# Loading the last three chunks of x by partition quadrant

## Chip, cores and metric

One core of one Trainium2 chip. The time is device microseconds of one execution, as the median of several; the kernel before takes 575.4 us.

## The reference, cut to what matters

```python
# x: (1, 384, 384, 384) bf16, dw: (1, 1, 384), pw: (384, 384)
out = x * dw[0, 0]                                  # k = 1: a depthwise scale per channel
return jnp.einsum('bhwc,cd->bhwd', out, pw)         # 147,456 rows times a 384 x 384 matrix
```

113 MB are read and 113 MB written. The kernel folds the scale into the weights, so each row of x needs only a transpose and a matrix product.

## The kernel before

The rows are cut into 288 supertiles of 512 rows. A chunk is a run of supertiles loaded by one transfer; most chunks have ten, the last group has 3, 2, 1, 1 and 1.

```python
head, tail = [[1, 1, 2, 2, 4]], [[6, 4], [3, 2, 1, 1, 1]]   # supertiles per chunk, by group
...
def load_x(t):
    g, i, off, first, L = chunks[t]
    dst = Xs[g % NR][:, 4 * off : 4 * (off + L), :]          # NR = 3 buffers
    rows = xf[512 * first : 512 * (first + L), :]
    if first + LONG < NS:                                     # LONG = 3, NS = 288
        src = rows.rearrange("(p s) c -> p (s c)", p=P)
        dst = dst.rearrange("p s c -> p (s c)")
    else:                                                     # the last three chunks
        src = rows.rearrange("(a k q) c -> q a k c", k=4, q=4)
    if i == 0 and g >= NR:                                    # buffer free?
        je = g_end[g - NR]
        nc.sync.wait_ge(s_t[je % 2][1], je // 2 + 1)
    nc.sync.dma_start(dst, src).then_inc(s_x[g % NR][i], 16)
```

VectorE transposes a supertile (two instructions), TensorE multiplies it (48 matmuls that each use 32 partitions, in twelve steps of four, one for each of four PSUM banks), ScalarE copies the result to an output buffer (VectorE helps with half of the very last), and SP stores each chunk once its last copy is done. The three last chunks have rows interleaved over the four quadrants of 32 partitions, so that their stores can write 3072 bytes in a piece; their loads then move 768-byte runs.

## Time and profile before

| | before |
|---|---|
| median of three runs | 575.39 us (575.29 to 575.57) |
| span of the profiled execution | 573.7 us |
| TensorE busy | 567.3 us, idle 0.1 us ahead of the main matmuls |
| DMA | 226.9 MB, 395 GB/s |

The lines that carry the reading stand in the prediction.

### The profile page before, as it was taken

The numbers are of one execution on the slowest core, as the hardware profiler recorded it, in microseconds if no ns is written. First come the engines' busy times: TensorE is split into PE (matmuls) and PEld (weight loads), VectorE is DVE, ScalarE is ACT, GpSimd is POOL, SyncE is SP. The second block draws the span as 40 slices with busy tenths as digits, with TensorE's granted clock in tenths as the row PEclk, the third lists the DMA queues.
The fourth block names the chain that finished last, engine by engine and source line by source line (L and its number), as shares of the span: only waits on it lengthen the run. The fifth ranks groups of instructions, "written<-read, shape, count | busy, mean of one in ns | idle before, by whom it ended". The sixth has DMA issues, their size and how long they took to land.

```text
span 573.7 us, 29706 instructions
## 1 busy us (share of the span) xinstructions
PE 567.3 (99%) x13869; PEld 414.9 (72%) x13869; DVE 509.3 (89%) x583; ACT 418.8 (73%) x296; POOL 0.9 (0%) x8
## 2 busy tenths in 40 slices
PE   8999999999999999999999999999999999999996
PEld 5777777777777777777777777777777777777774
DVE  6899999999999999999999999999999999999994
ACT  6777777777777777777777777777777777777775
POOL 0000000000000000000000000000000000000000
PEclk9999999999999999999999999999999999999999
DMA  8999999999999999999999999999999999994996
GB/s 324 432 409 417 430 397 430 444 424 422 399 408 416 384 397 436 398 383 395 432 398 384 395 429 390 393 401 429 402 385 419 401 390 397 425 394 149 402 408 251
DMA packets 25912, 226.88 MB, mean 395 GB/s; under 512 B 1197, under 2 KB 5678, under 8 KB 22062
## 3 DMA queue, kind: packets, MB, share of 16 engines
q1 hardware_dynamic: 25900, 226.79, 98.0%
q14 instruction: 9, 0.07, 0.0%
q8 instruction: 1, 0.02, 0.0%
q10 hardware_dynamic: 2, 0.00, 0.0%
HBM read 113.54 MB, written 113.25 MB: 395 GB/s over the span
## 4 chain that ended last, share of the span: by engine, by line
PE 98%; DMA 1%; ACT 0%; DVE 0%; issue 0%; SPq 0%
PE ps L166 97%; DMA pw_n<-in_pw_dram 1%; PE ps L216 1%; DMA out_dram<-O 0%; ACT O L307 0%; DVE O L304 0%; SPq L337 0%; SPq L100 0%
## 5 line engine op out<-in xcount | busy, mean ns | idle before, releaser
L166 PE MATMUL ps<-w_r,T 32*128 32x384 bf16 x13824 | 561.8, 321 | 0.1
L258 DVE STREAM_TRANSPOSE T<-X 128x384 uint32<-128x384 uint32 x576 | 506.2, 882 | 54.0 <-DMA X<-in_x_dram 2.4
L307 ACT CAST O<-ps 128x1536 bf16<-128x1536 f32 x288 | 413.5, 1436 | 147.9 <-PE ps L166 147.9
L166 PEld LDWEIGHTS ps<-w_r,T 32*128 32x128 bf16 x13824 | 412.9, 93 | 149.2 <-issue 0.7
L271 ACT CAST w_r<-ps 128x768 bf16<-128x768 f32 x5 | 3.7, 805 | 1.7 <-PE ps L216 1.6
L183 PE MATMUL ps<-zero 32*128 32x384 bf16 x24 | 2.6, 494 | 1.4 <-POOL zero L232 1.4
L304 DVE CAST O<-ps 128x768 bf16<-128x768 f32 x1 | 1.0, 958 | 3.0 <-DMA out_dram<-O 3.0
L216 PE MATMUL ps<-pw_n,sel_w 64*128 64x384 bf16 x18 | 3.0, 510 | 0.1
L183 PEld LDWEIGHTS ps<-zero 32*128 32x128 bf16 x24 | 0.7, 100 | 2.6 <-issue 2.6
L216 PEld LDWEIGHTS ps<-pw_n,sel_w 64*128 64x128 bf16 x18 | 1.2, 138 | 1.6 <-issue 1.2
L244 ACT ACT_TABLE_LOAD x1 | 1.3, 1283 | 1.5 <-SPq L100 1.5
L276 DVE TENSOR_REDUCE sel<-eye 128x64 f32<-128x128 bf16 x1 | 0.3, 290 | 1.8 <-POOL eye L234 1.8
L271 DVE CAST w_r<-ps 128x768 bf16<-128x768 f32 x1 | 1.0, 956 | 1.0 <-PE ps L216 1.0
L286 DVE TENSOR_SCALAR sel_w<-sel,dw_f 128x256 bf16<-128x256 f32 x3 | 0.9, 348 | 0.0
L283 DVE COPY dw_f<-ps 128x3 f32<-128x3 f32 x1 | 0.2, 161 | 0.8 <-PE ps L198 0.8
L198 PEld LDWEIGHTS ps<-ones,dw_row 1*128 1x128 bf16 x3 | 0.2, 98 | 0.2 <-issue 0.2
L244 ACT COPY warm<-warm 128x1 f32<-128x1 f32 x2 | 0.3, 188 | 0.0
L234 POOL TENSOR_SCALAR_AFFINE_SELECT eye<-ones 128x128 bf16<-128x128 bf16 x1 | 0.3, 292 | 0.1
L232 POOL MEMSET zero<- 128x192 uint32 x1 | 0.3, 258 | 0.0
L198 PE MATMUL ps<-ones,dw_row 1*128 1x1 bf16 x3 | 0.2, 159 | 0.0
L233 POOL MEMSET ones<- 128x128 bf16 x1 | 0.2, 204 | 0.0
L231 POOL MEMSET warm<- 128x3 f32 x1 | 0.1, 101 | 0.5 <-SPq L100 0.5
(4 smaller groups left out, 0.4 us busy)
## 6 DMA issues: line engine op xcount, KB each, us to landing
X<-in_x_dram SPq DMA_DIRECT2D x26, 3840.0 KB, 21.5
out_dram<-O SPq DMA_DIRECT2D x26, 3840.0 KB, 27.5
X<-in_x_dram SPq DMA_DIRECT2D x2, 1536.0 KB, 17.4
out_dram<-O SPq DMA_DIRECT2D x2, 1536.0 KB, 13.7
X<-in_x_dram SPq DMA_DIRECT2D x3, 768.0 KB, 8.8
out_dram<-O SPq DMA_DIRECT2D x3, 768.0 KB, 8.9
X<-in_x_dram SPq DMA_DIRECT2D x1, 2304.0 KB, 18.9
out_dram<-O SPq DMA_DIRECT2D x1, 2304.0 KB, 12.1
```

Source lines behind the costliest of these rows:

```text
L166: mm = nc.tensor.matmul(PS[s][:, q, :D], lhsT=Ts[s][32 * q : 32 * q + 32, b, par::2], rhs=w_r[32 * q : 32 * q + 32, b, par, :], start=(b, ...
L183: nc.tensor.matmul(PS[0][:, i, :D], lhsT=zero[32 * i : 32 * i + 32, 0:P], rhs=zero[32 * i : 32 * i + 32, :], start=True, stop=True, tile_p ...
L198: mm = nc.tensor.matmul(PS[1][:, 0, D + k : D + k + 1], lhsT=dw_row[:, P * k : P * k + P], rhs=ones[0:1, 0:1], start=True, stop=True,)
L216: mm = nc.tensor.matmul(PS[(k + 1) % 2][:, 2 * r + v, :D], lhsT=sel_w[64 * v : 64 * v + 64, k, r, :, :].rearrange("p q w -> p (q w)"), rhs ...
L232: nc.gpsimd.memset(zero[:].bitcast(U32), 0).then_inc(s_zero)
L234: nc.gpsimd.affine_select(out=eye[:], in_=ones[:], pattern=[[-1, P]], compare_op=mybir.AluOpType.is_equal, fill=0.0, base=0, channel_multi ...
L244: c = nc.scalar.copy(warm[:, s + 1 : s + 2], warm[:, 0:1])
L258: ins = nc.vector.transpose(out=Tw[:, 3 * h : 3 * h + 3], in_=Xw[:, :, j, 96 * h : 96 * h + 96].rearrange("p k (b w) -> p b k w", w=32),)
L271: o = nc.vector.tensor_copy(out, in_) if e == 0 else nc.scalar.copy(out, in_)
L286: nc.vector.tensor_scalar_mul(sel_w[:, k], sel[:].unsqueeze(2).to_broadcast([P, 2, 4, 32]), dw_f[:, k : k + 1]).then_inc(s_sw)
L304: e = nc.vector.tensor_copy(Ov[:, nq:4, j, :], PS[s][:, nq:4, :D])
L307: a = nc.scalar.copy(Ov[:, 0:nq, j, :], PS[s][:, 0:nq, :D])
```

## The change

Intent: each of the three loads used an access pattern with a dimension of 4 slowest; loading the quadrants one by one lets 32 partitions be slowest, so that all DMA engines share the work.

```diff
+    x_count = []
+    for t, (g, i, off, first, L) in enumerate(chunks):
+        n = 4 if first + LONG >= NS else 1
+        x_count.append(16 * n + max([... earlier count on the same semaphore ...], default=0))
...
             else:
                 src = rows.rearrange("(a k q) c -> q a k c", k=4, q=4)
-            nc.sync.dma_start(dst, src).then_inc(s_x[g % NR][i], 16)
+                for q in range(4):
+                    nc.sync.dma_start(dst[32 * q : 32 * q + 32], src[q]).then_inc(sem, 16)
...
-                    nc.vector.wait_ge(s_x[g % NR][i], 16 * sum(...))
+                    nc.vector.wait_ge(s_x[g % NR][i], x_count[t])
```

More of the change, by code (lines that the diff above doesn't have):

```diff
@@ L60 @@
     NT = len(chunks)
+    x_count = []
+    for t, (g, i, off, first, L) in enumerate(chunks):
+        n = 4 if first + LONG >= NS else 1
+        x_count.append(16 * n + max([x_count[u] for u in range(t) if chunks[u][0] % NR == g % NR and chunks[u][1] == i], default=0))
     g_end = [max(c[3] + c[4] for c in chunks if c[0] == g) - 1 for g in range(len(groups))]
@@ L104, in load_x @@
             rows = xf[512 * first : 512 * (first + L), :]
-            if first + LONG < NS:
-                src = rows.rearrange("(p s) c -> p (s c)", p=P)
-                dst = dst.rearrange("p s c -> p (s c)")
-            else:
-                src = rows.rearrange("(a k q) c -> q a k c", k=4, q=4)
+            sem = s_x[g % NR][i]
             if i == 0 and g >= NR:
@@ L112, in load_x @@
                 nc.sync.wait_ge(s_t[je % 2][1], je // 2 + 1)
-            nc.sync.dma_start(dst, src).then_inc(s_x[g % NR][i], 16)
+            if first + LONG < NS:
+                src = rows.rearrange("(p s) c -> p (s c)", p=P)
+                nc.sync.dma_start(dst.rearrange("p s c -> p (s c)"), src).then_inc(sem, 16)
+            else:
+                src = rows.rearrange("(a k q) c -> q a k c", k=4, q=4)
+                for q in range(4):
+                    nc.sync.dma_start(dst[32 * q : 32 * q + 32], src[q]).then_inc(sem, 16)
         def store(t):
@@ L256, in transposes @@
                 if h == 0 and j == 0:
-                    nc.vector.wait_ge(s_x[g % NR][i], 16 * sum(len(ls) > i for ls in groups[g % NR : g + 1 : NR]))
+                    nc.vector.wait_ge(s_x[g % NR][i], x_count[t])
                 ins = nc.vector.transpose(
```

## The prediction

> **What bounds the kernel now.** I read the page of the kernel before from the top: the busy table, then the costliest groups.
>
> ```profile
> PE 567.3 (99%) x13869; PEld 414.9 (72%) x13869; DVE 509.3 (89%) x583; ACT 418.8 (73%) x296; POOL 0.9 (0%) x8
> ...
> L166 PE MATMUL ps<-w_r,T 32*128 32x384 bf16 x13824 | 561.8, 321 | 0.1
> L258 DVE STREAM_TRANSPOSE T<-X 128x384 uint32<-128x384 uint32 x576 | 506.2, 882 | 54.0 <-DMA X<-in_x_dram 2.4
> L307 ACT CAST O<-ps 128x1536 bf16<-128x1536 f32 x288 | 413.5, 1436 | 147.9 <-PE ps L166 147.9
> ```
>
> The number to see is the last of the matmul row: TensorE was idle 0.1 us ahead of 13,824 matmuls. A busy figure alone would prove little, but ScalarE, which copies each result out, waited 147.9 us for these matmuls and for nothing else, while VectorE waited 2.4 us for x in the whole run. One supertile (512 rows of x, 48 matmuls) costs 561.8 / 288 = 1.951 us of TensorE, against 2 x 0.882 = 1.764 us of VectorE and 1.436 us of ScalarE. TensorE is the bound, from 7.2 us to the end.
>
> The change touches three loads late in the program, so next I read the stretch around them by windows, and the queue of the issuing engine (SP) in order of time. Columns of the windows: stretch, length, busy time and instruction count of each engine, granted clock, DMA share, GB/s.
>
> ```profile
> 0.00:518.00 518.00, 516.37 (x12621) 377.65 (x12625) 464.89 (x533) 380.59 (x269) 0.93 (x8) 1.00 1.00 406
> 518.00:530.00 12.00, 12.00 (x304) 8.83 (x300) 10.80 (x13) 8.63 (x6) 0.00 (x0) 1.00 0.37 118
> 530.00:560.00 30.00, 30.00 (x745) 22.11 (x741) 27.24 (x31) 22.32 (x16) 0.00 (x0) 1.00 0.98 397
> 560.00:562.00 2.00, 2.00 (x59) 1.49 (x52) 1.80 (x3) 1.49 (x2) 0.00 (x0) 1.00 0.39 152
> ```
>
> ```profile
> 512.29 0.71 SPq L113 DMA_DIRECT2D X<-in_x_dram  x1
> 513.05 8.79 SPq L113 DMA_DIRECT2D X<-in_x_dram  x1
> 521.89 4.44 SPq L113 DMA_DIRECT2D X<-in_x_dram  x1
> 526.38 4.41 SPq L128 DMA_DIRECT2D out_dram<-O  x1
> 535.37 0.39 SPq L128 DMA_DIRECT2D out_dram<-O  x1
> ```
>
> Here is the defect that the change repairs. The three loads of 384 KiB took SP 0.71, 8.79 and 4.44 us to issue, where other issues take 0.33 to 0.39, and they held the store behind them back to 526.38. For 12 us the DMA engines moved 118 GB/s at 0.37 of their capacity. TensorE was busy 12.00 of those 12.00 us all the same, at clock 1.00.
>
> **What the Trainium skill says.** "DMA: Bandwidth & Descriptors", section "Why a DMA increments its semaphore by 16 and not by 1": an SP transfer runs on k engines, k being the largest number up to 16 that divides the slowest dimension of both access patterns, and k engines post the completion. The old source has q, size 4, slowest, so k = 4; the new one has a = 32, its destination 32 partitions, so k = 16. The trace agrees on the 4: the page's DMA line counts the tiny packets.
>
> ```profile
> DMA packets 25912, 226.88 MB, mean 395 GB/s; under 512 B 1197, under 2 KB 5678, under 8 KB 22062
> ```
>
> The DMA view lists 38 loads of x, 38 stores, one of pw and one of dw: 78 transfers. If 74 post on 16 engines, the three loads on 4 and the one-row dw on 1, that is 74 x 16 + 3 x 4 + 1 = 1197, exactly the count. With k = 16 for the three it would be 1233.
>
> Same page, "Rules for kernel authors": two transfers to disjoint partition halves serialize because each already sprays over all engines; use one. Splitting would thus gain nothing if the old load had used 16 engines; it gains here only through k.
>
> "TensorE: Matmul & The Clock Gate", section "Wait — 56ns, not 53.3ns?": warm start-to-start is N / 2.4 GHz + 2.5 ns. With N = 384 that is 162.5 ns; and "TensorEngine Tiling (Array Packing)", "Key Properties", says that tiles operate independently, so four 32-row matmuls share one such interval. An estimate from the two pages: 48 / 4 x 162.5 = 1950 ns per supertile. The trace has 1951. The bound engine has no slack that a better transfer could return.
>
> **The change part by part.**
>
> Removed: three issues that take 0.71 + 8.79 + 4.44 = 13.94 us of SP, and about 4 us more (4.41 - 0.37) of the store behind them, which I take to be back-pressure of four full queues. A check: 393,216 bytes in 4.44 us is 89 GB/s, 22% of the 397 GB/s of a good stretch, close to 4 engines of 16.
>
> Added: twelve issues of 96 KiB, with the same bytes in the same 768-byte runs. At 0.35 us each (the usual issue of a load) that is 4.2 us, so SP is through at about 512.3 + 4.2 = 516.5; at 0.71 each, 520.8. I expect the first, as each transfer now puts 512 / 4 / 16 = 8 data packets on a ring, not 128. The three chunks are 1.18 MB: at 400 GB/s, 2.9 us, instead of about 12. SP saves about 10 us around 512 to 526. The tiny packets become (74 + 12) x 16 + 1 = 1377.
>
> Moved: the wait of VectorE counts 64 instead of 16 on each chunk's semaphore, still one wait. The store at 526.38 belongs to supertiles 250 to 259. The last copy-out begins at 569.00 and copies come every 1.95 us, so the one of supertile 259 began at 569.00 - 28 x 1.95 = 514.4 and ended at 515.8. That store goes out 5 to 10 us sooner.
>
> Who waited for any of this?
> - VectorE for x. The last transpose starts at 565.1, two per supertile, so the first of the last three chunks (supertile 285) is transposed from about 565.1 - 2 x 1.95 - 0.97 = 560.2. The slow stretch ended near 530: some 25 to 30 us to spare before the change.
> - ScalarE for the output buffer. Supertile 280 reuses the buffer that the delayed store empties. Its copy started at 569.00 - 7 x 1.95 = 555.4; the store landed 18.1 us after 526.38, at 544.5. Spare: 10.9 us.
> - The later stores, from 535.37 on, go out when a copy is done, so TensorE sets them.
>
> Saved on the path to the end: 0. Added: 0.
>
> The end itself: the last copy-out on VectorE starts at 569.01 and takes 0.96, the last store is issued at 570.06 and lands 2.3 us later, and the span closes at 573.7. None of these pieces changes if the last stores find empty queues. They did before: at 560 to 562 the DMA share was down to 0.39, so the backlog of the stall had been worked off 8 us before the last store. The change only empties it sooner.
>
> Sum: 575.39 + 0 = 575.4 us.
>
> **The rivals.**
>
> *The end was held by the store backlog, and comes sooner.* For it: SP is freed about 10 us earlier, and the page's chain names a store (2.46 us) near the end, for which the last VectorE copy is said to have waited 3.0 us. Against it: that copy waits for a store of three groups back, landed at 544.5, and for TensorE; it began within 0.01 us of the ScalarE copy that shows TensorE as its releaser. And the 0.39 share at 560. If true: 1 to 5 us less, 570 to 574.
>
> *Full-speed DMA beside the compute slows VectorE or TensorE.* For it: 118 GB/s becomes about 400 in this stretch. Against it: TensorE was fully busy and the copies came every 1.95 us at 118 and at 397 GB/s alike; and bytes only move from one time to another. If true for 12 us by a few per cent: 0.3 us more.
>
> *The twelve issues cost SP more than the three.* For it: nine more instructions; a queue that is full of the preceding loads could hold each up. Against it: even 1.2 us apiece would only equal the old 13.94 us, and nothing on the path waits for SP there. If they took 25 us, which nothing suggests, the store would slip past the copy at 555.4: up to some us more.
>
> *A straggling engine delays landing anyway.* The two ordinary loads just ahead landed 17.3 and 18.7 us after issue, so some queue holds old work. Then the split loads land near 530 whatever their width. Hidden too, but the gain in landing would be smaller than the gain in issue time.
>
> **Range and chances.** Three runs lay within 575.29 to 575.57. Predicted 575.4; I allow 0.5 us below and above for another chip or moment and for the small rivals: 574.9 to 575.9. Beyond 2% means under 563.9 or over 586.9. The first is about TensorE's own 561.8 us with a start and an end of 2 us together, and these take 7.2 and 4.7; the second needs a stall of 11 us that no part of the sum contains. Faster 0.01, same 0.98, slower 0.01.
>
> **What would show it right or wrong.** Right: twelve issues of about 0.35 us between 512 and 517, none above 1.5; no stretch near 118 GB/s from 518 to 530; the store now at 516 to 521; 1377 packets under 512 B; matmul idle time still 0.1 us; 1.95 us between copies; the last store still issued at 570.1. Wrong: idle time of TensorE beyond 0.5 us, a VectorE wait for x late in the run, a ScalarE wait for a store, or a last landing that moves by over 1 us. A count of 1233 or of 1197 would refute the engine arithmetic though not the time.

## More of the kernel before

One more line, from the waits of the issuing engine (SP), is the measure that will matter. Its columns: who waits, at which line, for whom, then microseconds in total, how often, and the longest.

```profile
SPq L141 <- DMA out_dram<-O: 2.0, 1, 2.0
```

It is SP's final wait for the stores to land, after the last one was issued at 570.06.

## The result

| | before | change |
|---|---|---|
| median of six runs | 575.44 us (575.29 to 576.12) | 577.56 us (577.10 to 577.62) |
| span of the profiled execution | 573.7 us | 575.4 us |
| ratio | | 1.0033, 95% interval 1.0020 to 1.0046 |

A ratio is the mean time of one kernel's fast runs over that of the other's of the same rounds, so it is not quite the ratio of the medians. The profiled execution of the change was its shortest, 577.10, which is why the spans differ by 1.7 us and the medians by 2.1. The change is slower by 2.1 us: within 2%, as the chances said, but clear of the noise and outside the predicted range of 574.9 to 575.9.

The profile after, in the same order as before. First the page's costliest group and its DMA line:

```profile
L173 PE MATMUL ps<-w_r,T 32*128 32x384 bf16 x13824 | 562.0, 321 | 0.2 <-ACT w_r L278 0.2
...
DMA packets 26092, 226.88 MB, mean 394 GB/s; under 512 B 1377, under 2 KB 5858, under 8 KB 22242
```

TensorE is as before. There are exactly the 1377 tiny packets foretold, so each quadrant does run on 16 engines. Next the windows and SP in order of time:

```profile
518.00:530.00 12.00, 12.00 (x304) 8.88 (x299) 10.87 (x13) 8.64 (x6) 0.00 (x0) 1.00 0.51 130
530.00:560.00 30.00, 30.00 (x746) 22.20 (x741) 27.07 (x32) 22.19 (x16) 0.00 (x0) 1.00 0.97 394
560.00:562.00 2.00, 2.00 (x57) 1.50 (x52) 1.81 (x3) 1.49 (x2) 0.00 (x0) 1.00 0.17 63
```

```profile
512.48 0.70 SPq L120 DMA_DIRECT2D X<-in_x_dram  x1
...
516.37 2.57 SPq L120 DMA_DIRECT2D X<-in_x_dram  x1
518.98 2.31 SPq L120 DMA_DIRECT2D X<-in_x_dram  x1
521.98 4.59 SPq L120 DMA_DIRECT2D X<-in_x_dram  x1
...
528.90 0.59 SPq L135 DMA_DIRECT2D out_dram<-O  x1
...
570.20 0.33 SPq L135 DMA_DIRECT2D out_dram<-O  x1
```

The stall between 518 and 530 is still there, at 130 GB/s instead of 118. Issues still block, up to 4.59 us, though the loads now use every engine, and the held store goes out at 528.90, not sooner than before (526.38) but 2.5 us later, though its own issue is shorter (0.59 us, not 4.41), so that it is out at 529.5 and not at 530.8. Then the end. The last store is issued at 570.20 instead of 570.06; what grew is SP's wait for the stores, and the time from issue to landing. The lines below are the same store in the DMA view (kilobytes, microseconds to landing), before and then after, and after's final wait:

```profile
out_dram<-O SPq DMA_DIRECT2D x1, 384.0 KB, 2.3
```

```profile
out_dram<-O SPq DMA_DIRECT2D x1, 384.0 KB, 3.8
```

```profile
SPq L148 <- DMA out_dram<-O: 3.5, 1, 3.5
```

So 1.5 us of the 1.7 us in the spans is a last landing that takes longer, and 0.14 us a copy that ends later.

Why does 384 KB take 1.5 us longer with nearly empty queues (a mean share of 0.17 at 560)? The trace also holds the time of every increment of a store's semaphore, the counter by which a transfer reports that it is done. Sixteen engines post one each, so a transfer has sixteen completion times. For the last store, relative to the start of the span (these are read from the trace's records, not from a view of the profile):

```
            first    15th     16th
before      572.20   572.34   572.37
change      572.35   572.51   574.05
```

Fifteen engines of the change finish within 0.2 us of those before. One is late. The records don't name the engines, but the late completions of the five stores of the last group, 569.33, 571.25, 572.20, 573.13 and 574.05, lie 1.92, 0.95, 0.93 and 0.92 us apart, in proportion to one engine's share of these stores (49 KB, then 24.6 KB each). One engine is working without a pause on a backlog of its own. Looking back over the run, the lag of the sixteenth completion behind the fifteenth, at the time of the first:

```
time, us    97    125   201   299   406   500
before      0.9   3.5   6.1   7.9   8.1   9.2
change      0.7   3.1   6.5   7.6   7.0   8.0
```

(For the change the columns lie within 1 us of these times.) The lag is not the change's doing. In both kernels one engine falls behind by 7 us between 97 and 299, and then stays some 7 to 9 us late until the traffic thins out.

**Theory T.** One engine of the sixteen is slow and brings a backlog to the end. Before, the three loads ran on four engines, and the slow one was not among them: it was spared 3 x 24.6 = 73.7 KB, a little over 3 us of its time at the 23 GB/s that it makes (147 KB in 6.35 us; an engine's mean share of the 394 GB/s from 530 to 560 is 24.6, so "slow" means some 6%), and just caught up with the last store. Spreading the loads over all engines gives it its sixteenth again. Of those 3 to 4 us, what exceeds its slack is seen at the end. Four engines are not free either: in the kernel before each of them carries 295 KB of the three chunks, and the store that lands at 553.60 there has five late completions (551.23, 552.15, 552.57, 552.59 and 553.60, the others by 550.73), where the change has one. They all catch up by the last store; which of the five is the last to do so, the records don't say.

**Rival R.** Twelve small transfers instead of three, with their issues and completions, cost the time.

### The profile page after: what moved, and what is told of

The parts are those of the page before. It is cut to its first block, busy times and chain, and to the rows that moved or that the text cites. A ratio compares the mean times of both kernels' runs of the same rounds, so it can differ in the third digit from the quotient of the medians.

```text
span 575.4 us, 29715 instructions
## 1 busy us (share of the span) xinstructions
PE 567.4 (99%) x13869; PEld 417.7 (73%) x13869; DVE 508.1 (88%) x583; ACT 419.2 (73%) x296; POOL 0.9 (0%) x8
## 2 busy tenths in 40 slices
DMA packets 26092, 226.88 MB, mean 394 GB/s; under 512 B 1377, under 2 KB 5858, under 8 KB 22242
## 4 chain that ended last, share of the span: by engine, by line
PE 98%; DMA 0%; ACT 0%; DVE 0%; issue 0%; POOL 0%; POOLq 0%; SPq 0%
PE ps L173 97%; PE ps L190 0%; DMA out_dram<-O 0%; PE ps L223 0%; ACT O L314 0%; DVE O L311 0%; ACT w_r L278 0%; POOL zero L239 0%; POOL warm L238 0%; PE ps L205 0%; POOLq L344 0%; SPq L105 0%
```

## The experiments

All kept TensorE's work as it is, and the last store was issued between 569.89 and 570.85 in all of them, so that at most 0.8 us of any loss comes ahead of it. "Last wait" is SP's final wait for the stores in the profiled execution, to be held against 2.0 us before and 3.5 us in the change.

### e1_slots: twelve transfers, on four engines

```diff
-                src = rows.rearrange("(a k q) c -> q a k c", k=4, q=4)
-                for q in range(4):
-                    nc.sync.dma_start(dst[32 * q : 32 * q + 32], src[q]).then_inc(sem, 16)
+                src = rows.rearrange("(a k q) c -> k q a c", k=4, q=4)
+                for k in range(4):
+                    nc.sync.dma_start(dst[:, k, :], src[k]).then_inc(sem, 16)
```

> The last three chunks in twelve transfers again, but one per slot k instead of one per quadrant, so that q (size 4) is the slowest dimension of the source and each should run on 4 engines: same bytes, same 768-byte runs, same number of issues as the change, result correct. Theory T (one DMA engine runs about 5 us behind the others in the tail, and the change put 3 x 24.6 KB more on it): as before, 575.4 us, last store landing about 2.3 us after issue; tiny packets 74 x 16 + 12 x 4 + 1 = 1233. Rival R (twelve small transfers and their completions cost the time): as the change, about 577.5.

Measured: 575.45 us (575.29 to 576.49), the kernel before 575.52 beside it, ratio 1.0001 (0.9989 to 1.0013); correct. 1233 tiny packets as expected.

```profile
SPq L148 <- DMA out_dram<-O: 2.0, 1, 2.0
```

Twelve transfers are free as long as they stay on four engines. As the cause by itself, R is out.

### e2_wide: three transfers, on sixteen engines

```diff
-                src = rows.rearrange("(a k q) c -> q a k c", k=4, q=4)
-                for q in range(4): ...
+                src = rows.rearrange("(k p) c -> p k c", p=P)
+                nc.sync.dma_start(dst, src).then_inc(sem, 16)
```

> One transfer per chunk as before, in 768-byte runs, but with the 128 partitions as the slowest dimension of the source, so that it runs on 16 engines; the rows land in other partitions, so the result is wrong on purpose in the last 1536 rows. Theory T: as the change, 577.3 to 577.7, last landing 3.5 to 4 us after issue; tiny packets 77 x 16 + 1 = 1233. Rival R (number of transfers): as before, 575.4.

Measured: 576.69 us (576.32 to 577.03), ratio 1.0018 (1.0006 to 1.0030); wrong in the last rows.

```profile
SPq L147 <- DMA out_dram<-O: 3.1, 1, 3.1
```

With no more transfers than before, sixteen engines are slower than four by 1.2 us. The direction is T's, R would have had 575.4; but the size is a miss, 0.6 us under what I had expected. The last experiments return to that.

### e3_fifteen: is it the sixteenth engine?

```diff
                 for q in range(4):
-                    nc.sync.dma_start(dst[32 * q : 32 * q + 32], src[q]).then_inc(sem, 16)
+                    for lo, hi in ((0, 30), (30, 32)):
+                        nc.sync.dma_start(dst[32 * q + lo : 32 * q + hi], src[q, lo:hi]).then_inc(sem, 16)
```

> As the change, but each quadrant in 30 + 2 partitions, which should run on 15 and on 2 engines, so that the sixteenth engine gets none of the three chunks; 24 transfers, result correct. Theory T with the slow engine being the sixteenth: as before, 575.4, last landing near 2.3 us, and the issues no longer blocked (all under 1 us); tiny packets 74 x 16 + 12 x 17 + 1 = 1389. T with another slow engine: as the change or slightly more, 577.5 to 577.8. Rival R: above the change, about 579.5, as there are 21 extra transfers and not 9.

Measured: 577.37 us (576.80 to 577.40); correct; 1389 tiny packets, so the engine counts are as supposed. The last wait was 3.9 us, and issues still blocked, up to 1.83 us. Sparing the sixteenth engine brings nothing, and 24 transfers are no worse than 12. It was a guess at the engine, and it missed.

### e4_two and e5_one: smaller doses

Two, then one, of the three chunks by quadrant; the rest in one transfer on four engines as before.

```diff
-        n = 4 if first + LONG >= NS else 1
+        n = 4 if NS - LONG <= first < NS - LONG + 2 else 1      # e5_one: + 1
...
+                if first < NS - LONG + 2:                        # e5_one: + 1
+                    (four transfers by quadrant)
+                else:
+                    nc.sync.dma_start(dst, src).then_inc(sem, 16)
```

> The first two of the three chunks by quadrant on 16 engines, the third in one transfer on 4 as before; a dose of two thirds. Theory T: the slow engine would be done at about 570.95 us if it never waited (574.05 minus 3.1 for 73.7 KB) and the last store cannot land before 572.4, so the first 1.4 us of extra work are free and the rest shows in full: two thirds of 3.1 is 2.1, so +0.6 to +1.1, 576.0 to 576.5. Rival R (cost in proportion to extra transfers, 6 of 9): +1.4, 576.8.

> Only the first of the three chunks by quadrant, the other two on 4 engines: a dose of one third. Theory T: with two thirds the last landing was 573.46 us, with all three 574.05, so one third should be at or a little above the floor of 572.4: 575.4 to 576.1. Rival R (3 extra transfers of 9): 576.1.

Measured: two chunks 576.56 us (576.31 to 576.92), last wait 3.1 us; one chunk 575.60 us (575.34 to 576.21) beside 575.34, last wait 2.0 us. Against the kernel before beside them the three doses cost 0.26, 1.04 and 1.9 to 2.3 us: the first third is free within the noise, the others are not. A slack followed by a rise is what T needs. But the interval of e5_one (ratio 0.9989 to 1.0017) also holds the 0.7 us that a cost per transfer would have given, so the doses alone do not separate the two; e1_slots does.

### f1_seven, f2_thirteen, f4_nine, g1_four, g2_five, g3_six: which engine, and does sparing it elsewhere help?

The change is kept whole. An earlier load, the 1152 KB first chunk of the last group, is cut by partitions so that it uses only some engines.

```diff
+                dst = dst.rearrange("p s c -> p (s c)")
+                for lo, hi in ((0, 124), (124, 128)) if first == NS - 8 else ((0, P),):
+                    nc.sync.dma_start(dst[lo:hi], src[lo:hi]).then_inc(sem, 16)
```

(124 + 4 is g1_four; the others are 125 + 3, 114 + 6 + 6 + 2, 119 + 7 + 2, 63 + 63 + 2 and 117 + 11; `n` for that chunk counts its pieces.) "DMA: Bandwidth & Descriptors", section "Why a DMA increments its semaphore by 16 and not by 1", adds that an SP transfer takes the lowest-numbered k engines. If so, each cut loads a known engine with a known share. The counts of tiny packets (1369 to 1385) agree with the number of engines supposed for each piece; which engines they are, no record shows.

> The change kept whole; instead an earlier load, of 1152 KB (the first chunk of the last group), is cut into 119 + 7 + 2 partitions, which should run on 7, 7 and 2 engines, so that engines 8 to 16 get none of it. Theory T: if the slow engine is one of those nine, it loses 73.7 KB, which is what the change gave it, and the time is back at 575.4 with a last landing near 2.3 us, though the last three chunks are still split. If the slow engine is the fifth to seventh, it gets 84 KB more and the time rises to 580 to 581. Rival R (number of transfers, or the splitting itself): 577.5 or a little more.

> As the seven-engine run, but the load in 117 + 11 partitions on 13 and 11 engines. Theory T: slow engine the fourteenth to sixteenth: 575.4; slow engine earlier: 577.5 to 578.3, as it gets some 10 to 20 KB more than in the change. Rival R: 577.5.

> As the seven-engine run, but the load in 63 + 63 + 2 partitions on 9, 9 and 2 engines. Theory T: slow engine the tenth or later: 575.4; slow engine the eighth or ninth: it gets 131 KB instead of 73.7, 57 KB more, at 23 GB/s 2.5 us, so 579.5 to 580.5. Rival R: 577.5.

> The change kept whole, and the 1152 KB load in 124 + 4 partitions, both on 4 engines, so that only the first four carry it. Seven, nine and thirteen engines all made it slower, with one late engine alone, which leaves the fifth to seventh engine as the slow one, if a transfer takes the lowest-numbered engines. Theory T: that engine loses 73.7 KB, as much as the change gave it: back to 575.3 to 576.0, last landing 2.3 to 2.8 us, although the three chunks stay split on 16 engines. Rival R2 (any cutting of loads here, and any further transfer, costs time; the seven-engine run was slow for that): 577.5 or above.

> As the four-engine run, with 125 + 3 partitions on 5 and 3 engines. Theory T: slow engine the fifth: 236 KB instead of 73.7, 162 KB more, 7 us: 584 to 586; slow engine the sixth or seventh: 575.3 to 576.0.

> As the four-engine run, with 114 + 6 + 6 + 2 partitions on 6, 6, 6 and 2 engines. Theory T: slow engine the seventh: 575.3 to 576.0; the sixth: 194 KB instead of 73.7, 120 KB more, 5.2 us: 582 to 584; the fifth: the same 582 to 584.

Measured, with the share of the fifth engine in that load (one partition is 9216 bytes; 117 over 13 engines and 11 over 11 put 9 + 1 = 10 on it, and so on):

| run | engines used | on the fifth engine | median us (range) | last wait us |
|---|---|---|---|---|
| g1_four | 4 | 0 | 575.75 (575.23 to 577.66) | 4.2, see below |
| the change (g4_change) | 16 | 8 x 9216 = 74 KB | 577.60 (576.54 to 577.84) | 4.3 |
| f2_thirteen | 13, 11 | 10 x 9216 = 92 KB | 578.72 (578.26 to 580.30) | 4.7 |
| f4_nine | 9, 9, 2 | 14 x 9216 = 129 KB | 580.26 (579.72 to 580.52) | 6.2 |
| f1_seven | 7, 7, 2 | 18 x 9216 = 166 KB | 581.67 (581.10 to 582.66) | 7.4 |
| g3_six | 6, 6, 6, 2 | 21 x 9216 = 194 KB | 581.90 (581.17 to 582.27) | 8.1 |
| g2_five | 5, 3 | 25 x 9216 = 230 KB | 583.37 (582.54 to 584.59) | 8.7 |

g4_change ran beside the g runs; the f runs are from another chip, where the change made 577.35 later (h3_change). The lines for the largest of these, g2_five, and for f1_seven:

```profile
SPq L150 <- DMA out_dram<-O: 8.7, 1, 8.7
```

```profile
SPq L150 <- DMA out_dram<-O: 7.4, 1, 7.4
```

Every cut from thirteen engines down to five costs more time, and the cut to four brings it back. No count of pieces gives that order, and one engine's load does: the fifth carries a part of the load in all cuts but that to four, and the time follows its bytes. Between the change and g2_five, on one chip, 156.7 KB cost 5.77 us, 27 GB/s; between the change (577.35 on that chip) and f1_seven 92.2 KB cost 4.32 us, 21 GB/s. The smallest step is out of proportion: the 18 KB of f2_thirteen cost 1.4 us there, which bytes alone do not account for. In f1_seven's completion times, fifteen engines are done with the last store by 572.70 and one at 578.06. My sizes for single cuts were off by up to 0.7 us either way (f1_seven and f2_thirteen above the stated range, g2_five and g3_six below).

g1_four's profiled execution was its one long run, 577.66; the other four lie between 575.23 and 575.81. Its completion times show several late engines, the last done at 574.62; they may be the four that carry 295 KB each of that one load. So it was repeated with less burden on these.

### i1_four_small: the same relief with a smaller load

As g1_four, with the 768 KB load (`first == NS - 5`) cut into 124 + 4 partitions.

> The change kept whole, and the 768 KB load before the three chunks (not the 1152 KB one) in 124 + 4 partitions on the first four engines. Theory T: the slow engine loses 49 KB, 2.1 us at 23 GB/s, against the 1.7 us of the change's profile, so the time is back at 575.3 to 575.9 and the last landing at 2.3 to 2.6 us; the four engines carry 147 KB more each instead of 221. Rival R2 (further cutting only adds): 577.5 or above.

Measured: 575.71 us (575.54 to 575.98), the kernel before 575.59, ratio 0.9999 (0.9986 to 1.0013); correct.

```profile
SPq L150 <- DMA out_dram<-O: 2.7, 1, 2.7
```

The three chunks are still split on sixteen engines, there is one transfer more than in the change, and the loss is gone. The last landing took 3.0 us in the profiled run, the slowest of its five: one engine still at 572.94 beside the others at 572.2; I had expected 2.3 to 2.6.

### g4_change, h1_wide12, h2_wide, h3_change: what is left over

Why did e2_wide cost only 1.2 us? The change and the wide run were repeated, and the wide pattern was issued as twelve transfers, one per slot:

```diff
+                src = rows.rearrange("(k p) c -> k p c", p=P)
+                for k in range(4):
+                    nc.sync.dma_start(dst[:, k, :], src[k]).then_inc(sem, 16)
```

> The change itself once more, beside the others on one chip. 577.1 to 577.7, last landing 3.5 to 4 us, 15 of 16 engines done with the last store 1.5 us earlier.

> Twelve transfers of 96 KB, each over all 128 partitions on 16 engines in 768-byte runs; the rows land in other partitions, so the result is wrong on purpose in the last 1536 rows. Bytes on the slow engine as in the change; tiny packets 74 x 16 + 12 x 16 + 1 = 1377. If the number of transfers on the slow engine makes the gap to the wide run: as the change, 577.3 to 577.7. If the 32-partition shape makes it: as the wide run, 576.5 to 576.9.

> The wide run once more (three transfers on 16 engines, wrong on purpose). If the gap is real: 576.5 to 576.9, some 0.9 us under the change on the same chip; if it was the chip: within 0.3 us of the change.

> The change once more beside them: 577.4 to 577.7, as on two occasions before.

Measured: the change 577.60 (576.54 to 577.84) and 577.35 us (576.96 to 577.53); the wide run again 576.44 (576.22 to 576.80); twelve wide transfers 576.71 (576.15 to 577.19). The gap of 0.9 us on one chip is real, as the ranges do not overlap. By the completion times, the late engine took from the end of the load before to the end of the three chunks 3.36 us in h2_wide, 4.05 in h3_change and 4.07 in h1_wide12: twelve small transfers cost it 0.7 us more than three for the same bytes. That speaks for the number of transfers on the slow engine. But h1_wide12's profiled execution was its longest, and its median lies nearer to the wide run. So the split of the gap between the number and the 32-partition shape stays open.

## Why the prediction was wrong

Right in the prediction: TensorE sets the pace (idle 0.2 us, copies still 1.95 us apart), the old loads ran on four engines and the new ones on sixteen (1377 tiny packets in the change, and 1233, 1257 and 1389 in e1_slots, e5_one and e3_fifteen, each as the arithmetic has it), no transpose and no copy waits late in the run, the last store is issued at 570.2 (foretold 570.1), and the result stays far within 2%.

Wrong, by its steps:

1. *"None of these pieces changes if the last stores find empty queues. They did before: at 560 to 562 the DMA share was down to 0.39, so the backlog of the stall had been worked off."* This is the step that failed. The share is a mean over sixteen engines. In the change it is lower still, 0.17, and yet one engine reached the end with a backlog of 1.5 us. A landing is the last of sixteen completions, and I had looked at the average of sixteen queues. In the sum, "Added: 0" should have been the slow engine's new work, 4.06 us for the three chunks by its completion times, less its slack. The slack is not known well. Worked back from the change's own end it is 2.4 us (574.05 - 4.06 = 569.99, against the floor of 572.4 that the last copy sets), so this sum gives the 1.7 us of the spans by construction and checks nothing. In e4_two the same working gives 1.8 us (2.84 us of new work, last landing 573.46), and in e5_one 1.04 us of new work used all of it (its late engine was done with the last store but one at 571.44, and 0.93 more is 572.4).

2. *"I expect the first"*, twelve issues of 0.35 us, done at 516.5, and the store 5 to 10 us sooner. They blocked up to 4.59 us each and the store went out at 528.90. The reading of the old issues as back-pressure of four full queues was wrong, or not the whole of it: in e2_wide, with sixteen engines and three transfers, two issues took 4.05 and 9.70 us, and the held store went out at 526.70, as before (526.38). What blocks them is open. The late engine with its 8 us of old work may have a part, but it is not needed: in the kernel before a store at 16.67 took 14.56 us to issue ("0.33 to 0.39" for the other issues overlooked it), and the lag from 23 to 34 us was 0.1 to 0.6 us. All of this is off the path to the end, as the prediction said of SP's time there. Wrong too, and off the path, was the expectation that the stretch at 118 GB/s would vanish; it stayed, at 130.

3. *The rival "A straggling engine delays landing anyway"* had seen the right thing, in two loads that landed 17 and 19 us after issue, and then applied it to loads alone, where it is hidden. The same engine serves the last store. The rivals for a slower result gave 0.3 us or "up to some us" for other reasons.

4. The use made of the skill's rule against splitting, cited in the prediction (the gain comes only through k), counted a larger k as pure gain. Fewer engines were the better choice here, because the load had 25 us to spare and the slow engine had little (the first chunk of the three was free within the noise).

What is shown: the loss follows the bytes on one engine, in the three chunks and in two other loads. That this engine is the fifth rests on the skill's statement on which engines k selects, with which all cuts agree; they ran on three chips. Why it is slow is open.

No version beat the kernel before. e1_slots, e5_one, g1_four and i1_four_small all end at its level, as the last copy and one store set a floor there.

## What to carry to other kernels

A transfer lands when its slowest engine lands, so look for the sixteenth completion, not for the mean DMA share, before calling a queue empty. A mark of it in the profile is that equal stores take unequal times to land: the last three before, of 384 KB each, took 3.3, 2.6 and 2.3 us, since one of the sixteen completions came 0.71, 0.24 and 0.03 us after the others. These three times could have been read before the change was made. Near the end of a kernel, a load with time to spare may be better on few engines, as here, if that spares the one that the last store will wait for. Changing how a hidden transfer is spread can move the end, even when nothing waits for that transfer.

## What the Trainium skill lacked or had wrong

- "DMA: Bandwidth & Descriptors", "Latency and other measured facts", calls engines 7 and 15 usually slower and ties that, as a best guess, to software descriptor rings. Here all bulk transfers are issued from SP, and the slow one is the fifth of sixteen (4 in the page's count), if k selects the lowest-numbered: it fell 7 us behind between 97 and 299 us and was 9.2 us late at 500 us, and moved 21 to 27 GB/s at the margin.
- The same page, "Rules for kernel authors", advises using all 16 engines. For three hidden loads of 384 KB, 16 engines cost 1.0 to 1.2 us more than 4 in one transfer each (h2_wide and e2_wide; the interval of the first, 0.9997 to 1.0027, just includes no loss), and 1.9 to 2.3 us more in four transfers each (medians against the kernel before beside them). The page has no word on loads that share an engine with a later, critical store.
- "Perfetto Trace Analysis" shows a descriptor buffer that can fill within the time of an issue, but no page that I read says how deep it is or for how long an issue on SP can block: issues of 8.79 and 4.44 us before and of up to 4.59 us in the change, beside a usual 0.35.
- "DMA: Bandwidth & Descriptors", "Rules for kernel authors", has no number for splitting by partitions. Here, for the same bytes on 16 engines, twelve transfers by quadrant took 577.35 us and three wide ones 576.44 on one chip, and the slow engine 4.05 us against 3.36; the row layouts differ too.
